# Attention and a gated two-layer network on one core: the last 64 keys of each pair of heads as four products in quarters of the TensorE array

## The chip, the cores and the metric

One core of a Trainium2 chip runs the kernel. The metric is device time in microseconds (us) of one execution, the median of several runs. TensorE does the matrix products (PE in the profile, PEld its weight loads), VectorE is DVE, ScalarE is ACT, GpSimd is POOL, and SyncE (SP) issues the transfers.

## What is computed

Attention over 4 batches, 12 heads, 448 tokens and 64 dimensions a head, with scores capped by tanh, then a network with a cosine gate on the 1792 tokens of 768 features:

```python
scores = scale * np.matmul(q, k.transpose(0, 1, 3, 2))
scores = cap * np.tanh(scores / cap)
scores = scores - np.max(scores, axis=-1, keepdims=True)
attn = np.exp(scores)
attn = attn / (np.sum(attn, axis=-1, keepdims=True) + 1e-09)
out = np.matmul(attn, v)
# heads side by side: x of 1792 x 768
h = x @ w_in                 # 768 x 2048
g = h * np.cos(h)
return g @ w_out             # 2048 x 768
```

## The kernel before

Heads go in pairs: the 64 dimensions of head 0 of a pair lie on partitions 0 to 63, those of head 1 on 64 to 127. Two pairs (a = 0, 1) make a quad q, and there are 12 quads (0 to 11). For each pair one transfer (L320; L125 and L127 for the first quad) brings keys and queries as `qk`, another (L325) the values as `v`. The layout is made on the host in `_layout`.

The 448 keys are cut into groups g of 128, 128, 128 and 64. For the first three, `scores` (L333) makes for each head one product of 64 rows by 128 columns with all 448 queries: the two heads stand in the upper and the lower half of the array's rows, and write two PSUM banks of a tile `pair`. The last 64 keys of both pairs share one tile, `rest`: pair a writes partitions 64a to 64a + 63, head h writes bank h. `scores_rest` (L342) makes its four products each over all 128 rows. For this the 64 keys are stored as 128 columns with zeros: columns 384 to 447 hold head 0 on the upper 64 partitions and zeros below, columns 448 to 511 hold head 1 on the lower 64 and zeros above (KD = 512), so that each product takes the queries of both heads and the zeros remove the wrong one.

From there ScalarE takes the tanh out of PSUM (L352: `t` for the first groups, `late` for rest and the third group) and the exponential in place (L367). VectorE adds the exponentials of a pair up (`sum`, L406, L409, L413). TensorE multiplies them with the values into two tiles `single` (`values`, L426: four column strips of 32, one for each pair and head) and sums them over the keys (`sums`, L435, into a tile `rest`). VectorE then transposes the sums (L446), inverts them (L453), spreads them (L459), scales the result (L463) and splits it into a high and a low part (L466, L469). L426 of the next quad writes the `single` tiles that L463 has read.

In attention the order of every engine is written out: PLAN gives each part a time in a cycle of 13.8, all calls of all quads are sorted by it and made in that order. TensorE does in each quad: scores of pair 0 (groups 0 and 1), `scores_rest`, the values of the rest group of the quad before, scores of pair 1 (groups 0, 1), the sums and the values of group 2 of the quad before, scores of group 2 of both pairs, values of groups 0 and 1. Both `pair` tiles are used in turn; `rest` has one buffer.

During attention the first weights of the network are prepared, in quads 2 to 9: transfers into `w` (L232), and on VectorE in one quad L239, L243, L247, L254, in the next L257, L261 and L476 (the last one in three of them). The network (from L201 on) follows: products of float32r parts into `single` and `pair`, the gate on ScalarE and VectorE, the output product (L611) added to `acc` (L623).

Of the kernel before, what the change touches and what calls it, by code (L numbers as in the profile page):

```python
# [19 lines left out]
B, H, S, D = 4, 12, 448, 64  # L20
# [59 lines left out]
EARLY_AT = dict(no_sign=2.4, scale=2.9, cap=3.4, shift=3.9, tail_bits=16.2, sign_bit=17.1, load=17.2, high=18.1, low=19.8, load_rest=20.0)  # L80
BUSY = 6, 5
PAD = 80
KD = 512
QK = KD + S
Q = slice(KD, QK)
RAW = QK + 128 * NG
# [198 lines left out]
class Heads:  # L285
# [50 lines left out]
    def scores_rest(self, q):  # L336

        ps = self.ps[q] = self.banks.rest()
        for h in range(2):
            for a in range(2):  # L340
                x = self.qk[q, a]
                self.nc.tensor.matmul(ps[64 * a:64 * a + 64, h, 0:S], lhsT=x[:, 384 + 64 * h:448 + 64 * h],  # L342
                                      rhs=x[:, Q], start=True, stop=True)

    def t(self, q, a, g):

# [396 lines left out]
def _layout(inputs):  # L743
    import numpy as np

    q, k, v = inputs['q'], inputs['k'], inputs['v']
    qkv = np.zeros((B, NPAIR, 128, RAW), dtype=q.dtype)
    kt = k.transpose(0, 1, 3, 2).reshape(B, NPAIR, 128, S)
    qkv[..., 0:384] = kt[..., 0:384]
    qkv[:, :, 0:64, 384:448] = kt[:, :, 0:64, 384:448]  # L750
    qkv[:, :, 64:128, 448:512] = kt[:, :, 64:128, 384:448]
    qkv[..., KD:QK] = q.transpose(0, 1, 3, 2).reshape(B, NPAIR, 128, S)
    vp = v.reshape(B, NPAIR, 2, S, D)
    vv = np.zeros((B, NPAIR, 128, NG, 2, D), dtype=v.dtype)
    vv[:, :, :, 0:3] = vp[:, :, :, 0:384].reshape(B, NPAIR, 2, 3, 128, D).transpose(0, 1, 4, 3, 2, 5)
    vv[:, 0::2, 0:64, 3] = vp[:, 0::2, :, 384:448].transpose(0, 1, 3, 2, 4)
    vv[:, 1::2, 64:128, 3] = vp[:, 1::2, :, 384:448].transpose(0, 1, 3, 2, 4)
    qkv[..., QK:RAW] = vv.reshape(B, NPAIR, 128, RAW - QK)
    qkv = qkv.reshape(B * NPAIR, 128, RAW)
    w_in = inputs['moe_w_in'].reshape(NQUAD, 4, 2, 32, DFF).transpose(0, 2, 1, 3, 4)  # L760
    w_in = w_in.reshape(KC, 128, NF, 128).transpose(2, 1, 0, 3).reshape(NF, 128, DM)
    w_out = inputs['moe_w_out'].reshape(NF, 128, DM)
    w_in = np.ascontiguousarray(w_in).view(np.int64)
    w_out = np.ascontiguousarray(w_out).view(np.int64)
    return {'qkv': qkv, 'cap': np.asarray(inputs['cap']).reshape(1), 'w_in': w_in, 'w_out': w_out}
# [24 lines left out]
```

## Time and profile before

| | before |
|---|---|
| time, median of 3 runs | 653.33 us (650.8 to 653.75) |
| profiled execution | 653.35 us |
| its span, first to last instruction | 651.5 us |
| TensorE busy | 640.2 us, 98% |
| VectorE busy | 501.7 us, 77% |
| ScalarE busy | 320.0 us, 49% |
| granted TensorE clock, mean | 0.994 of full |

The profile is one execution. Busy time is that in which an engine has an instruction running; the records of TensorE overlap each other, so the distance between starts tells more than the duration of one. An f32 product shows as two records and two weight loads. "Idle before" is the time in which an engine stood still before an instruction, with what ended it in brackets. Attention ends at about 183 us, the network takes the rest.

### The profile page before, as it was taken

The page shows a single profiled execution, that of the slowest core. Times are in us where ns is not written, and L with a number is a line of the kernel's source. Part 1 is how long each engine was busy: PE and PEld are TensorE (multiplying, and loading weights), DVE is VectorE, ACT ScalarE, POOL GpSimd, SP SyncE. Part 2 cuts the span into 40 slices and gives each one's busy share as a digit, 9 for nine tenths or more (in the row PEclk, how much of TensorE's full clock was granted, in tenths as well). Part 3 has the DMA queues.
Part 4 walks back from the last instruction along what each step waited for, and adds up shares of the span by engine and source line. Part 5 has one row for each costly group of instructions (what it writes and reads, how often), then busy time and mean ns, then how long its engine had stood idle before and what let it go on. Part 6 is the DMA issues. An engine that isn't in the chain of part 4 may idle for free.

```text
span 651.5 us, 9197 instructions
## 1 busy us (share of the span) xinstructions
PE 640.2 (98%) x3755; PEld 498.3 (76%) x3755; DVE 501.7 (77%) x755; ACT 320.0 (49%) x385; POOL 62.1 (10%) x39
## 2 busy tenths in 40 slices
PE   7999999999999999999999999999999999999995
PEld 2333333333469999998999999899999999998995
DVE  1599999997768887877887878777778778777664
ACT  4999999999824333334333333333343333333220
POOL 0001011000011111111111111111111111111000
PEclk9999999999999999999999999999999999999998
DMA  7044342444001122111111221111112211110223
GB/s 262 7 151 140 127 142 94 153 144 144 1 0 50 50 67 79 49 49 48 49 50 51 70 74 50 48 50 49 49 49 66 80 50 49 48 49 1 97 98 150
DMA packets 18497, 49.42 MB, mean 76 GB/s; under 512 B 2192, under 2 KB 2448, under 8 KB 18448
## 3 DMA queue, kind: packets, MB, share of 16 engines
q1 hardware_dynamic: 18448, 48.77, 22.2%
q8 instruction: 31, 0.51, 0.3%
q14 instruction: 18, 0.15, 0.1%
HBM read 43.25 MB, written 5.51 MB: 75 GB/s over the span
## 4 chain that ended last, share of the span: by engine, by line
PE 93%; DVE 3%; ACT 1%; issue 1%; DMA 0%; POOL 0%; ACTq 0%
PE single L201 32%; PE pair L611 24%; PE single L426 12%; PE rest L611 10%; PE pair L333 9%; PE rest L342 3%; PE rest L435 2%; PE pair L201 1%; DVE gl L588 1%; DMA capt<-in_cap_dram 0%; DVE acc L621 0%; DVE y L575 0%; DVE y L582 0%; PE rest L106 0%; POOL wi2l L269 0%
## 5 line engine op out<-in xcount | busy, mean ns | idle before, releaser
L579 ACT ACTIVATE y<-y,angles 128x384 f32<-128x384 f32 (+1 forms) x63 | 42.3, 671 | 161.5 <-DVE y L576 161.5
L623 DVE TENSOR_TENSOR acc<-pair,acc 128x768 f32<-128x768 f32 x70 | 66.7, 953 | 14.3 <-PE pair L611 14.2
L333 PE MATMUL pair<-qk 64*128 64x448 f32 x264 | 58.6, 562 | 0.0
L585 ACT CAST gh<-y 128x384 fp32r<-128x384 f32 (+1 forms) x63 | 35.8, 567 | 45.6 <-DVE y L582 45.6
L582 DVE TENSOR_TENSOR y<-single,y 128x384 f32<-128x384 f32 (+1 forms) x62 | 38.5, 621 | 25.4 <-ACT y L579 25.4
L567 ACT ACTIVATE v<-single,angles 128x384 f32<-128x384 f32 (+1 forms) x62 | 39.0, 629 | 29.0 <-PE single L201 28.9
L236 ACT ACTIVATE u<-w 128x768 f32<-128x768 f32 x28 | 25.1, 895 | 53.9 <-POOL wo2l L269 10.0
L333 PEld LDWEIGHTS pair<-qk 64*128 64x128 f32 x264 | 22.7, 186 | 36.2 <-issue 20.1
L352 ACT ACTIVATE t<-pair,inv 128x896 f32<-128x896 f32 x48 | 45.7, 1004 | 5.8 <-PE pair L333 5.3
L251 DVE TENSOR_SCALAR u<-u 128x768 f32<-128x768 f32 x28 | 15.7, 561 | 39.0 <-ACT u L236 38.9
L367 ACT ACTIVATE t<-t,capt 128x1792 f32<-128x1792 f32 x24 | 42.8, 1783 | 0.4
L406 DVE TENSOR_TENSOR sum<-t 128x896 f32<-128x896 f32 x24 | 26.1, 1088 | 21.2 <-ACT t L367 21.2
L576 DVE SCALAR_TENSOR_TENSOR y<-v,y 128x384 f32<-128x384 f32 (+1 forms) x63 | 39.3, 624 | 2.2
L588 DVE TENSOR_TENSOR gl<-y,gh 128x384 fp32r<-128x384 f32 (+1 forms) x63 | 38.8, 616 | 2.5 <-ACT gh L585 2.5
L426 PE MATMUL single<-late,v 128*32 128x448 f32 x368 | 40.7, 542 | 0.0
L575 DVE SCALAR_TENSOR_TENSOR y<-v,single 128x384 f32<-128x384 f32 (+1 forms) x62 | 38.4, 619 | 2.1
L426 PE MATMUL single<-t,v 128*32 128x448 f32 x368 | 39.2, 546 | 0.0
L570 DVE TENSOR_SCALAR v<-v 128x384 f32<-128x384 f32 (+1 forms) x63 | 24.4, 387 | 15.3 <-ACT v L567 15.2
L201 PE MATMUL single<-xh,wi2l 128*128 128x512 f32 (+1 forms) x96 | 34.9, 363 | 0.0
L201 PE MATMUL single<-xh,wi2h 128*128 128x512 f32 (+1 forms) x96 | 34.8, 363 | 0.0
L201 PE MATMUL single<-xh,wi3h 128*128 128x512 f32 (+1 forms) x96 | 34.7, 362 | 0.0
L201 PE MATMUL single<-xh,wi3l 128*128 128x512 f32 (+1 forms) x96 | 34.7, 362 | 0.0
(151 smaller groups left out, 1571.7 us busy)
## 6 DMA issues: line engine op xcount, KB each, us to landing
w<-in_w_in_dram SPq DMA_DIRECT2D x32, 384.0 KB, 3.6
w<-in_w_out_dram SPq DMA_DIRECT2D x32, 384.0 KB, 3.6
qk<-in_qkv_dram SPq DMA_DIRECT2D x22, 480.0 KB, 4.9
v<-in_qkv_dram SPq DMA_DIRECT2D x23, 256.0 KB, 3.9
out_dram<-acc SPq DMA_DIRECT2D x13, 384.0 KB, 2.3
w<-in_qkv_dram SPq DMA_DIRECT2D x2, 240.0 KB, 3.8
second<-in_qkv_dram SPq DMA_DIRECT2D x1, 480.0 KB, 5.5
out_dram<-acc SPq DMA_DIRECT2D x2, 192.0 KB, 3.9
```

The lines of the kernel that those rows point to most:

```text
L201: nc.tensor.matmul(h[:, 0:n], lhsT=w[:, ks], rhs=x[:, k, toks], start=(k == 0 and i == 0), stop=(k == KC - 1 and i == 2))
L333: self.nc.tensor.matmul(ps[:, h, 0:S], lhsT=x[mine, 128 * g:128 * g + 128], rhs=x[mine, Q], start=True, stop=True)
L352: self.nc.scalar.activation(out, ps[:, :, 0:S], AF.Tanh, scale=self.inv)
L367: self.nc.scalar.activation(t, t, AF.Exp, scale=self.capt)
L426: self.nc.tensor.matmul(self.acc[q][e][o], lhsT=self.v[q, a][:, g, d], rhs=t, start=(g == first), stop=(g == last), tile_position=(0, o.st ...
L567: m.nc.scalar.activation(self.v, self.h, AF.Identity, bias=m.quarter, scale=1.0 / (2.0 * math.pi))
L576: m.nc.vector.scalar_tensor_tensor(self.y, self.v, -TWO_PI_LO, self.y, op0=ALU.mult, op1=ALU.add)
L579: self.m.nc.scalar.activation(self.y, self.y, AF.Sin, bias=self.m.half_pi)
L582: self.m.nc.vector.tensor_mul(self.y, self.h, self.y)
L588: self.m.nc.vector.tensor_sub(self.result(1), self.y, self.result(0))
L611: m.nc.tensor.matmul(y[:, e, 0:HALF], lhsT=x[:, j, toks], rhs=w[:, HALF * e:HALF * e + HALF], start=(j == 0 and k == 0), stop=(j == GF - 1 ...
L623: m.nc.vector.tensor_add(acc, y[:, e, 0:HALF], acc)
```

## The change

`scores_rest` takes for head h only the 64 partitions of that head, for the keys and for the queries, and names the place in the array: rows 64h, columns 64a. The keys of a pair are stored once, without zeros (KD = S = 448), so a pair's keys and queries are 896 words a partition instead of 960. The order of the calls stays.

```diff
-KD = 512
+KD = S
 QK = KD + S
 Q = slice(KD, QK)
 RAW = QK + 128 * NG
...
         for h in range(2):
             for a in range(2):
-                x = self.qk[q, a]
-                self.nc.tensor.matmul(ps[64 * a:64 * a + 64, h, 0:S], lhsT=x[:, 384 + 64 * h:448 + 64 * h],
-                                      rhs=x[:, Q], start=True, stop=True)
+                x, mine = self.qk[q, a], slice(64 * h, 64 * h + 64)
+                self.nc.tensor.matmul(ps[64 * a:64 * a + 64, h, 0:S], lhsT=x[mine, 384:448], rhs=x[mine, Q],
+                                      start=True, stop=True, tile_position=(64 * h, 64 * a))
...
-    qkv[..., 0:384] = kt[..., 0:384]
-    qkv[:, :, 0:64, 384:448] = kt[:, :, 0:64, 384:448]
-    qkv[:, :, 64:128, 448:512] = kt[:, :, 64:128, 384:448]
+    qkv[..., 0:KD] = kt
```

## Rows read from the trace of the kernel before

**Rows 1.** Page, part 1: busy time, share of the span, instructions.
```profile
PE 640.2 (98%) x3755; PEld 498.3 (76%) x3755; DVE 501.7 (77%) x755; ACT 320.0 (49%) x385; POOL 62.1 (10%) x39
```

**Rows 2.** Page, part 4: the chain that ended last, shares by line.
```profile
PE single L201 32%; PE pair L611 24%; PE single L426 12%; PE rest L611 10%; PE pair L333 9%; PE rest L342 3%; PE rest L435 2%; PE pair L201 1%; DVE gl L588 1%; DMA capt<-in_cap_dram 0%; DVE acc L621 0%; DVE y L575 0%; DVE y L582 0%; PE rest L106 0%; POOL wi2l L269 0%
```

**Rows 3.** Stretches: length, busy PE, PEld, DVE, ACT, POOL (instructions), clock, DMA share, GB/s.
```profile
77.40:91.40 14.00, 14.00 (x110) 4.60 (x106) 13.14 (x19) 12.96 (x12) 2.68 (x1) 1.00 0.32 105
91.40:105.30 13.90, 13.90 (x108) 4.57 (x104) 12.81 (x20) 12.90 (x11) 0.00 (x0) 1.00 0.48 173
...
161.10:175.00 13.90, 13.90 (x108) 4.58 (x104) 10.69 (x16) 12.92 (x11) 0.00 (x0) 1.00 0.01 2
...
190.00:640.00 450.00, 449.68 (x2425) 427.91 (x2424) 348.96 (x537) 158.67 (x244) 52.85 (x29) 1.00 0.17 56
```

**Rows 4.** Timeline, TensorE: start, duration (us), line, out<-in, shape, count [idle before].
```profile
100.48 1.77 PE L333 MATMUL pair<-qk 64*128 64x448 f32 x8
102.19 3.21 PE L426 MATMUL single<-t,v 128*32 128x448 f32 x32
...
107.04 1.73 PE L342 MATMUL rest<-qk 128*64 128x448 f32 x8
108.69 1.71 PE L426 MATMUL single<-late,v 128*32 128x448 f32 x16
...
112.04 0.96 PE L435 MATMUL rest<-sum,one 128*32 128x448 f32 x8
...
114.43 1.77 PE L333 MATMUL pair<-qk 64*128 64x448 f32 x8
```

**Rows 5.** Timeline, TensorE, L342 in the first quad.
```profile
9.74 0.59 PE L342 MATMUL rest<-w 128*64 128x448 f32 x1
9.74 0.59 PE L342 MATMUL rest<-second 128*64 128x448 f32 x1
10.16 0.54 PE L342 MATMUL rest<-w 128*64 128x448 f32 x1
...
10.54 0.54 PE L342 MATMUL rest<-w 128*64 128x448 f32 x1
```

**Rows 6.** Timeline, TensorE, L426 in the first quad (values of two pairs).
```profile
20.05 0.54 PE L426 MATMUL single<-t,u 128*32 128x448 f32 x2
20.07 0.54 PE L426 MATMUL single<-t,v 128*32 128x448 f32 x2
20.43 0.54 PE L426 MATMUL single<-t,u 128*32 128x448 f32 x2
```

**Rows 7.** TensorE's weight loads: L426 in the timeline; L342 by line (min/median/max ns).
```profile
103.34 0.13 PEld L426 LDWEIGHTS single<-t,v 128*32 128x32 f32 x4 [0.25 <-issue]
...
L342 PEld LDWEIGHTS rest<-qk x88: 132/137/137, 23.4 to 163.6; 128*64 128x64 f32 x88
```

**Rows 8.** Timeline, ScalarE: its two waits in one quad.
```profile
108.81 1.01 ACT L352 ACTIVATE late<-rest,inv 128x896 f32<-128x896 f32 x1 [0.50 <-PE rest L342]
...
115.50 1.01 ACT L352 ACTIVATE late<-pair,inv 128x896 f32<-128x896 f32 x1 [0.37 <-PE pair L333]
```

**Rows 9.** Timeline, VectorE, in a quad that ends a weight piece.
```profile
100.83 1.16 DVE L463 TENSOR_TENSOR x<-single,s 128x448 f32<-128x448 f32 x2
...
111.53 1.09 DVE L406 TENSOR_TENSOR sum<-t 128x896 f32<-128x896 f32 x1
113.06 0.65 DVE L446 STREAM_TRANSPOSE s<-rest 128x448 f32<-128x448 f32 x1 [0.44 <-PE rest L435]
...
114.78 1.16 DVE L463 TENSOR_TENSOR x<-single,s 128x448 f32<-128x448 f32 x2
```

**Rows 10.** Timeline, VectorE, in the quad before, which begins a weight piece.
```profile
95.80 0.56 DVE L239 TENSOR_SCALAR u<-w 128x768 int32<-128x768 int32 x1 [0.64 <-DMA w<-in_w_out_dram]
...
99.12 0.65 DVE L446 STREAM_TRANSPOSE s<-rest 128x448 f32<-128x448 f32 x1
```

**Rows 11.** Timeline, ScalarE, in the first quad.
```profile
11.51 1.01 ACT L352 ACTIVATE late<-rest,inv 128x896 f32<-128x896 f32 x1 [0.52 <-PE rest L342]
```

## Prediction

> **What bounds the kernel now.** I read the busy shares first: TensorE is busy 98% of the span [rows 1]. A busy matmul engine proves little, so next comes the chain that ended last: the reader should see there that nearly all of it is TensorE's own lines, and that the line which the change rewrites, L342, holds 3% of the span [rows 2]. The table of stretches says where another engine stands close behind [rows 3]. In attention, from 21.6 to 175.0, TensorE is busy for the whole of every stretch, and ScalarE is busy some 12.9 of 13.9 us; VectorE is at 12.8 to 13.1 in the quads that also prepare weights, and at 10.7 in the last ones. In the second half (190 to 640) TensorE is busy 449.68 of 450 us, and VectorE 349. So whatever attention saves moves the second half forward whole, and the question is only what attention saves.
>
> Then one quad on TensorE in order of time [rows 4]. From the third pair of scores of one quad (100.48) to that of the next (114.43) it takes 13.95 us, the same for quads 1 to 11 within 0.01 us. Within it, no line shows an idle time: TensorE sets this beat alone. L342 takes 107.04 to 108.69 = 1.65 us of it, as 8 records (each f32 product shows as two).
>
> **The new product.** The first quad has its two key loads under different names, so its records stand apart [rows 5]: the product from pair 0 and that from pair 1 start together at 9.74, and their second halves at 10.16; then come 10.54 and so on. So the two column halves of the array run side by side, four rounds of two records, 0.38 us a round. The first round is 0.42, and the last, up to the next line's start, 0.47: 0.42 + 2 x 0.38 + 0.47 = 1.65, as in the steady quad. After the change each product needs 64 rows only, so the two heads can run side by side too: two rounds of four records. L426 does four records side by side already, in four column strips (20.05 and 20.07 hold two each, the next round starts 0.38 later) [rows 6], and L333 two in row halves: 8 records in 1.70 us [rows 4]. Both directions at once is what no row shows. Taken together they leave 0.42 + 0.47 = 0.89 instead of 1.65: two rounds less, 0.75 us a quad. At the worst that rows price, all four products follow each other (8 rounds, 1.5 us more a quad); at the best the entry and exit extras (0.04 and 0.09) go too, another 0.1. I take 0.75, since each direction alone keeps the full round of 0.38 with as many records as there are tiles. The head is also the index of the PSUM bank in this line, so the two row halves write different banks, as in L333, and nothing new meets there.
>
> A page speaks against this. In L426 the four products of a round share all the rows, and yet the weights of the next round load while they run: four loads of together 0.13 us, begun 0.25 us after the last ones [rows 7], with the rounds still 0.38 apart. The Trainium skill, "TensorE: Matmul & The Clock Gate", section "Part 3: Packing small matmuls — row/col tiling", says that a weight load overlaps running matmuls only if its row group differs. By that rule the two products of one head would not overlap; the sum by it is the slower rival below, and the sum by rows is the 0.75. The trace does not agree with the rule for column strips.
>
> **What else changes.** The key loads shrink by a fifteenth (from 960 to 896 words a row). TensorE waits for none of them in attention, so this is worth nothing on the path; it can only help a late weight transfer behind them. The tile order, the plan and all waits of the engines stay. No instruction is added or taken away; L342 keeps its 8 records, 4 products and their loads.
>
> **What comes next on the path.** TensorE's beat becomes 13.95 - 0.75 = 13.20 us. ScalarE waits 0.50 us for L342 and 0.37 for the third pair of scores in each quad [rows 8]; the first wait goes (L342's result comes 0.75 earlier, ScalarE is free 0.50 earlier), and the second shrinks as ScalarE gains 0.50 and TensorE 0.75. It needs no more than 13.95 - 0.87 = 13.08, less than 13.20: not the bound, by 0.1 us.
>
> VectorE is the nearest. In a quad that ends a weight piece [rows 9], L463 ends at 100.83 + 1.16 = 101.99 and lets L426 start at 102.19. From there VectorE has no idle time until L406 ends at 111.53 + 1.09 = 112.62; it then waits 0.44 for the sums (L435) and starts L446 at 113.06, 1.02 after L435 began at 112.04. From L446 to the next end of L463 (114.78 + 1.16 = 115.94) takes 2.88. With the wait gone, its beat is 13.95 - 0.44 = 13.51, that is 0.31 more than TensorE's new one. Three quads are like this. In the four that begin a piece VectorE is busy 0.3 us less in a stretch 0.1 us shorter [rows 3], so about 13.25, 0.05 over. The 0.20 us between L463's end and L426 is slack, spent once; some of it is the way of the signal, so I take 0.15. VectorE thus takes back 3 x 0.31 + 4 x 0.05 - 0.15 = 0.98 us over the kernel. Once L426 waits for L463, all of TensorE's queue waits behind it.
>
> In one quad VectorE also waited 0.64 us for a weight transfer, so that L446 at 99.12 came without any wait for TensorE [rows 10]. That transfer is issued behind the values of the quad before, so it keeps its distance to the beat: there the quad cannot get shorter by more than the slack, and 0.58 of its 0.75 are lost. This depends on when one transfer lands: 0 if it lands as early as in the other quads, and with smaller transfers ahead of it. I take 0.4.
>
> The first quad is set by ScalarE, which waits 0.52 us for L342 [rows 11]. What it gains there lies between 0 and 0.52, since TensorE may hold it up later in the same quad. I take 0.3, about the middle.
>
> **The sum.** 11 x 0.75 = 8.25, plus 0.3 for the first quad, minus 0.98 and 0.4: 7.2 us. The profiled execution took 653.35 us (651.5 of span and 1.85 around it); the median of the runs is 653.33, so nothing is to be corrected. 653.35 - 7.2 = 646.2.
>
> **The rivals.**
> First, only two tiles run at a time, so four rounds stay: the change does not do what it says. For it speaks only that no row shows both directions at once; against it, that each works fully by itself. 653.3 us, within 0.5% of before for sure. Chance 0.08.
>
> Second, on the other side: products that share their rows follow each other, weights included. Then each row half has four records of 0.38, each with its own load of 0.14 (the median of L342's loads, [rows 7]). 4 x 0.52 = 2.08, plus 0.09 at the exit, 2.17 against 1.65: 0.52 more in each of 12 quads, 6.2 us, 659.6. It decides as soon as a group takes longer than 1.65 us, that is with fewer than two products at a time. Against it: the four strips of L426, which share their rows and run together [rows 6, 7]. That is the rule of the page named above. Chance 0.05.
>
> Third, VectorE takes back far more: every quad that begins a weight piece gets the late transfer (4 x 0.58 = 2.3 in place of 0.2 + 0.4), and the extras at the change of tile shape grow by 0.1 in each quad (1.2). 7.2 - 1.7 - 1.2 = 4.3: 649.0. For it: VectorE's 13.51 is over the new beat already. Against it: only one of the four waited. Chance 0.09.
>
> The forecast itself gets the rest, 0.78.
>
> **How the numbers follow.** The forecast's own range goes from all gains and no loss (8.25 + 0.52 + 11 x 0.1 = 9.9, 643.5) to the loss of the transfer in a second quad (647). To hold 8 in 10 the range takes in the third case too: 643.5 to 649.5, leaving out the first two rivals and a little more. A measurement of this kernel can tell about 0.5%, 3.3 us, from no change; faster by more is below 650.1. Forecast and third rival lie below it: 0.86. Within 0.5% is the first rival and a few mixtures: 0.09. Slower is the second: 0.05.
>
> **What would show it.** In the profile after, L342's eight records should start in two rounds of four, 0.4 us apart, with 0.9 us to the next line; four rounds would be the first rival, more than 1.65 us the second. ScalarE's 0.50 before the tanh of L342 should be gone. The wait of VectorE's L446 for L435 should vanish in the weight quads and stay in the last two quads. TensorE should show short waits for L463 at the start of L426 in quads 3 to 9 and nowhere else; quads 10 and 11 should take 13.20 us each. The second half should keep its length. If the last quads too are longer than 13.2, or TensorE waits for ScalarE, the account of the engines behind it was wrong.

## The result and the profile after

The changed kernel takes 643.88 us (median of 4 runs, 642.73 to 643.93); the kernel before, in the same measurement, 652.08 (650.8 to 653.75). The ratio is 0.987, with a 95% interval of 0.985 to 0.989. The interval leaves out 1, so it is faster, and by a little more than the 7.2 us of the forecast: the medians are 8.2 us apart. The profiled executions, which the account below adds up, are 653.35 and 643.93 us, 9.4 apart; their spans are 651.47 and 642.14, 9.3 apart.

TensorE in one quad of the changed kernel, as in [rows 4] (start, duration, line, out<-in, shape, count):

```profile
95.73 1.77 PE L333 MATMUL pair<-qk 64*128 64x448 f32 x8
97.43 3.21 PE L426 MATMUL single<-t,v 128*32 128x448 f32 x32
...
102.28 0.98 PE L342 MATMUL rest<-qk 64*64 64x448 f32 x8
103.19 1.71 PE L426 MATMUL single<-late,v 128*32 128x448 f32 x16
...
108.93 1.77 PE L333 MATMUL pair<-qk 64*128 64x448 f32 x8
110.64 0.58 PE L426 MATMUL single<-t,v 128*32 128x448 f32 x4
```

L342 now takes 102.28 to 103.19 = 0.91 us instead of 1.65, and the quad 95.73 to 108.93 = 13.20 instead of 13.95. There is still no idle time on TensorE in this quad. The first quad shows the rounds one by one, as in [rows 5]; the timeline of TensorE again:

```profile
9.75 0.59 PE L342 MATMUL rest<-w 64*64 64x448 f32 x1
9.75 0.59 PE L342 MATMUL rest<-second 64*64 64x448 f32 x1
9.76 0.59 PE L342 MATMUL rest<-w 64*64 64x448 f32 x1
9.77 0.59 PE L342 MATMUL rest<-second 64*64 64x448 f32 x1
10.17 0.54 PE L342 MATMUL rest<-w 64*64 64x448 f32 x1
...
10.66 1.77 PE L333 MATMUL pair<-second 64*128 64x448 f32 x8
```

Four records start within 0.02 us, the second four 0.42 later, and the next line 0.49 after that. So the quarters do run four at a time. ScalarE's wait for L342 [rows 8] is gone, and its second wait is down from 0.37 to 0.25 (ScalarE's timeline):

```profile
103.44 1.01 ACT L352 ACTIVATE late<-rest,inv 128x896 f32<-128x896 f32 x1
...
110.00 1.01 ACT L352 ACTIVATE late<-pair,inv 128x896 f32<-128x896 f32 x1 [0.25 <-PE pair L333]
```

VectorE, in the quad that answers to [rows 9] and in the one before it (VectorE's timeline):

```profile
91.31 0.57 DVE L239 TENSOR_SCALAR u<-w 128x768 int32<-128x768 int32 x1
...
96.29 1.16 DVE L463 TENSOR_TENSOR x<-single,s 128x448 f32<-128x448 f32 x2
...
106.46 0.56 DVE L476 CAST wo0h<-u 128x768 fp32r<-128x768 f32 x1
106.93 1.08 DVE L406 TENSOR_TENSOR sum<-t 128x896 f32<-128x896 f32 x1
107.93 0.65 DVE L446 STREAM_TRANSPOSE s<-rest 128x448 f32<-128x448 f32 x1
...
109.64 1.16 DVE L463 TENSOR_TENSOR x<-single,s 128x448 f32<-128x448 f32 x2
...
122.78 1.16 DVE L463 TENSOR_TENSOR x<-single,s 128x448 f32<-128x448 f32 x2
```

L446 no longer waits for the sums: VectorE is behind TensorE in this quad, as forecast. But TensorE does not wait for it. The pair of L463 ends at 109.64 + 1.16 = 110.80, and L426 had started at 110.64, before that end. In the kernel before it started 0.20 after it ([rows 4, 9]). This row contradicts the prediction's account of what L426 waits for, and the experiments start from it. L239, which waited 0.64 for its transfer [rows 10], shows no wait here.

The second half kept its length: from the first product of the network to the end of the last addition it is 470.6 us before (from 175.06) and after (from 166.59). Within it the engines are as busy as before (stretches: length, busy PE, PEld, DVE, ACT, POOL, clock, DMA share, GB/s; compare [rows 3]):

```profile
180.00:630.00 450.00, 449.71 (x2424) 427.99 (x2423) 347.79 (x535) 159.82 (x246) 53.62 (x29) 1.00 0.17 56
```

### The profile page after: what moved, and what is told of

It reads as the page before. It is cut to its first block, busy times and chain, and to the rows that moved or that the text cites. A ratio compares the mean times of both kernels' runs of the same rounds, so it can differ in the third digit from the quotient of the medians.

```text
span 642.1 us, 9197 instructions
## 1 busy us (share of the span) xinstructions
PE 631.8 (98%) x3755; PEld 495.9 (77%) x3755; DVE 500.5 (78%) x755; ACT 318.5 (50%) x385; POOL 61.9 (10%) x39
## 4 chain that ended last, share of the span: by engine, by line
PE 93%; DVE 3%; ACT 2%; issue 1%; DMA 0%; POOL 0%; ACTq 0%
PE single L201 32%; PE pair L611 24%; PE single L426 12%; PE rest L611 10%; PE pair L333 9%; PE rest L435 2%; PE rest L342 2%; PE pair L201 1%; DVE gl L588 1%; DMA capt<-in_cap_dram 0%; ACT t L352 0%; DVE acc L621 0%; DVE y L575 0%; DVE y L582 0%; PE rest L106 0%
## 5 line engine op out<-in xcount | busy, mean ns | idle before, releaser
L333 PE MATMUL pair<-qk 64*128 64x448 f32 x264 | 58.6, 562 | 0.0
L333 PEld LDWEIGHTS pair<-qk 64*128 64x128 f32 x264 | 22.8, 186 | 36.1 <-issue 19.8
L426 PE MATMUL single<-late,v 128*32 128x448 f32 x368 | 40.7, 542 | 0.0
L406 DVE TENSOR_TENSOR sum<-t 128x896 f32<-128x896 f32 x24 | 26.0, 1085 | 18.1 <-ACT t L367 18.1
L426 PE MATMUL single<-t,v 128*32 128x448 f32 x368 | 39.6, 548 | 0.0
L201 PE MATMUL single<-xl,wi3h 128*128 128x512 f32 (+1 forms) x96 | 34.7, 362 | 0.0
```

Source lines behind the costliest of these rows:

```text
L201: nc.tensor.matmul(h[:, 0:n], lhsT=w[:, ks], rhs=x[:, k, toks], start=(k == 0 and i == 0), stop=(k == KC - 1 and i == 2))
L333: self.nc.tensor.matmul(ps[:, h, 0:S], lhsT=x[mine, 128 * g:128 * g + 128], rhs=x[mine, Q], start=True, stop=True)
L426: self.nc.tensor.matmul(self.acc[q][e][o], lhsT=self.v[q, a][:, g, d], rhs=t, start=(g == first), stop=(g == last), tile_position=(0, o.st ...
```

## The experiments

**Products alone, products in another order.** The first kernel keeps the old layout with zeros and the transfers of 960 words (its edits against the changed kernel, the lines of `_layout` left out):

```diff
-KD = S
+KD = 512
...
-                self.nc.tensor.matmul(..., lhsT=x[mine, 384:448], rhs=x[mine, Q],
+                self.nc.tensor.matmul(..., lhsT=x[mine, 384 + 64 * h:448 + 64 * h], rhs=x[mine, Q],
```

> The products in quarters alone: keys are stored with the zeros as before (960 words a row, KD = 512), and the products take only their 64 rows. If the whole gain is TensorE's two rounds a quad: L342's group 0.91 us, 13.20 us a quad, the network begins at 166.6, the time within 1 us of the changed kernel (643.9). If the smaller transfers carry part of it: VectorE's L239 waits again for a weight transfer (0.4 to 0.6 us in one quad) and the slack of L463 ahead of L426 shrinks there by as much; the time still moves only when that slack (0.37 us at the least in the changed kernel) is used up, so at most 0.3 us.

Measured: 643.55 us (641.11 to 643.93), ratio 0.985 (0.982 to 0.988); L342's group 0.91 us; from the values of the second quad to those of the last, 30.99 to 163.01, ten quads of 13.20; no wait of L239. The whole gain is the products'; the smaller transfers carry none of it that can be seen.

The second exchanges the loops:

```diff
-        for h in range(2):
-            for a in range(2):
+        for a in range(2):
+            for h in range(2):
```

> The four products in another order: pairs outside, heads inside, so that products of one column half and different row halves follow each other. If a tile of the array runs as soon as its own predecessor is done, whatever stands between: L342's group stays at 0.91 us, two rounds of four. If four at a time needs products with the same rows to be neighbours: more than two rounds, 1.3 us (three) to 1.65 us (four), and 0.4 to 0.75 us more a quad, 4.5 to 9 us in all.

Measured: 643.52 us, L342's group 0.91 us. The four run at a time in both orders. TensorE's timeline in the first quad of that kernel:

```profile
10.35 0.59 PE L342 MATMUL rest<-w 64*64 64x448 f32 x2
10.37 0.59 PE L342 MATMUL rest<-second 64*64 64x448 f32 x2
10.78 0.54 PE L342 MATMUL rest<-w 64*64 64x448 f32 x2
```

This run also gave, by chance, a late transfer like the one that the prediction priced at 0.58 us, though L239 waits 0.22 for it here and not 0.64. VectorE's timeline, and under it TensorE's:

```profile
91.18 0.57 DVE L239 TENSOR_SCALAR u<-w 128x768 int32<-128x768 int32 x1 [0.22 <-DMA w<-in_w_out_dram]
...
109.49 1.16 DVE L463 TENSOR_TENSOR x<-single,s 128x448 f32<-128x448 f32 x2
```
```profile
96.95 3.21 PE L426 MATMUL single<-t,v 128*32 128x448 f32 x32
...
110.17 3.31 PE L426 MATMUL single<-t,v 128*32 128x448 f32 x32
...
123.47 1.71 PE L426 MATMUL single<-t,v 128*32 128x448 f32 x16
```

The transfer came later than in the changed kernel, VectorE fell further behind (L426 starts 0.48 before the end of the pair of L463: 109.49 + 1.16 = 110.65 against 110.17), and the quads at 96.95 and 110.17 took 13.22 and 13.30. So this late transfer costs some 0.1 us, because there is slack to take the rest of it.

**How much slack, and where.** L463 is one row of two instructions, one for each of the two `single` tiles. If L426's first products wait only for the tile they write, the slack counts from the end of the first L463: in the changed kernel and before, where VectorE is on time, 0.73 us (the second ends 0.53 later, and 0.20 before L426). To use the slack up, VectorE gets more work in the four quads that begin a weight piece:

```diff
+        at(CYCLE * cycle + EARLY_AT["no_sign"], calls["no_sign"])
```

> L239 (0.56 us on VectorE, with its step 0.59) made twice in each of the four quads that begin a weight piece. Theory: L426's first products wait only for the first of the two L463, so TensorE has 0.73 us of slack, of which some 0.03 is the way of the signal. VectorE's beats are 13.17 + 0.59 in these quads and 13.35 in the three that end a piece with L476, against 13.20: 4 x 0.56 + 3 x 0.15 - 0.70 = 2.0 us later at the start of the network. The prediction's account (slack 0.15, beats 13.25 + 0.59 and 13.51): 4 x 0.64 + 3 x 0.31 - 0.15 = 3.3 us. If VectorE doesn't bound these quads at all: 0.

Measured, TensorE's timeline with the values of the second, a middle and the last quad, then VectorE's at the middle one:

```profile
31.01 3.21 PE L426 MATMUL single<-t,v 128*32 128x448 f32 x32
...
71.20 3.31 PE L426 MATMUL single<-t,v 128*32 128x448 f32 x32 [0.41 <-DVE x L463]
...
165.15 3.21 PE L426 MATMUL single<-t,v 128*32 128x448 f32 x32
```
```profile
70.53 1.16 DVE L463 TENSOR_TENSOR x<-single,s 128x448 f32<-128x448 f32 x2
```

The same two rows of the changed kernel:

```profile
31.42 3.21 PE L426 MATMUL single<-t,v 128*32 128x448 f32 x32
...
163.45 3.21 PE L426 MATMUL single<-t,v 128*32 128x448 f32 x32
```

The ten quads took 165.15 - 31.01 = 134.14 against 132.03: 2.1 us longer, where the theory said 2.0 and the prediction's account 3.3. (The prediction's slack of 0.15 with the theory's beats, which are nearer to those measured, would give 4 x 0.56 + 3 x 0.15 - 0.15 = 2.5, so the length alone does not decide on the slack; the moment at which L426 starts does.) Now TensorE waits for L463, and even then it starts at 71.20, 0.49 before the pair ends (70.53 + 1.16 = 71.69): the first of the two ended at 71.15. The whole kernel took 645.21 us in its one run.

To see that it is the tile written first that counts, the two L463 were exchanged on top of this:

```diff
-    ("norm_scale", (0,), 21.2),
-    ("norm_scale", (1,), 21.8),
+    ("norm_scale", (1,), 21.2),
+    ("norm_scale", (0,), 21.8),
```

> As e4_no_sign_twice, and the two L463 of a quad in the other order, so that the tile that L426 writes first is freed by the second of them. Theory (the slack is that of the tile written first): the slack falls from 0.73 to 0.20 us, so the network begins 0.5 us later than in e4_no_sign_twice, 2.5 later than in the changed kernel. If L426 waits for both L463 anyhow, as the prediction took it, the order makes no difference: as e4_no_sign_twice within 0.1 us.

Measured: 164.92 - 30.85 = 134.07, the same as before the exchange (the whole kernel 645.70 us in its one run). The theory's 0.5 us did not come. TensorE's timeline and then VectorE's at the middle quad:

```profile
71.03 3.31 PE L426 MATMUL single<-t,v 128*32 128x448 f32 x32 [0.40 <-DVE x L463]
```
```profile
70.35 1.16 DVE L463 TENSOR_TENSOR x<-single,s 128x448 f32<-128x448 f32 x2
```

L426 again starts 0.48 before the pair ends (71.51), as without the exchange. The likely reason is that the pool, which hands out the PSUM banks of the tiles, gave the bank that is freed first to the tile that is written first, so that the two tiles changed banks from quad to quad. No trace names the banks; the next run tests it. So this run does not tell the two accounts apart. With each tile held on its own bank:

```diff
-        return self.pool.tile([128, 512], F32, name="single", tag="single")
+        self.made = 1 - getattr(self, "made", 1)
+        return self.pool.tile([128, 512], F32, name="single", tag=f"single{self.made}", bufs=1)
```

> As e3_twice_swapped, but each of the two single tiles keeps its PSUM bank from quad to quad (in e3_twice_swapped the pool gave the bank freed first to the tile written first, whichever it was, so the swap changed nothing). Now L426's first products write the bank that the second L463 frees. Theory (the slack is that of the bank written first): 0.20 us in place of 0.73, L426 never starts before the end of the second L463, and the quads from the first L426 to the last take together 0.5 us more than in e4_no_sign_twice (2.1 us over ten times 13.20 there, 2.6 here). If L426 needs both tiles anyhow: no difference from e4_no_sign_twice.

Measured (this kernel has one line more, so L426 is L427, L463 is L464 and L333 is L334), TensorE's timeline and then VectorE's at the middle quad:

```profile
28.49 3.22 PE L427 MATMUL single<-t,v 128*32 128x448 f32 x32
...
69.20 3.33 PE L427 MATMUL single<-t,v 128*32 128x448 f32 x32 [0.36 <-PE pair L334]
...
163.10 3.25 PE L427 MATMUL single<-t,v 128*32 128x448 f32 x32
```
```profile
67.95 1.15 DVE L464 TENSOR_TENSOR x<-single,s 128x448 f32<-128x448 f32 x2
```

163.10 - 28.49 = 134.61: 0.5 us more than in e4, as the theory said. L427 now starts at 69.20, 0.10 after the second L464 (67.95 + 1.15 = 69.10), never ahead of it. (The whole kernel took 643.30 us in its one run; that is shorter than e4's because its second quad starts some 2.5 us earlier, for which see the last section.) The row names L334 as what ended the wait, but L334 is the line whose products had just run on TensorE itself; the end of L464 is what fits the start. So the slack is that of the bank written first, shown from both sides: 0.73 us from the end of the first L463, of which 0.05 stayed unused in e4.

**A step further.** Of TensorE's beat of 13.20, what is not rounds of products is the extra time at each change of tile shape. The values of the rest group can stand beside the sums, so that three groups in column strips follow each other:

```diff
-    ("values", (3,), 14.4),
+    ("values", (3,), 18.4),
```

This is e5; in e6 the time is 18.55, just behind the sums.

> The changed kernel again, on the same chip as the two that follow: 643.9 us.

> A step further: the values of the rest group are moved from behind L342 to just ahead of the sums (time 18.4 in place of 14.4), so that three groups of products in column strips follow each other and one change of tile shape a quad falls away. The group takes 1.64 us alone, four rounds within others 1.50: 0.14 us a quad, 1.6 us in all, if TensorE sets the beat (13.06). VectorE's beats of 13.35 and 13.17 in seven quads are over that by 0.29 and 0.11: 3 x 0.29 + 4 x 0.11 = 1.3, less 0.7 of slack, so 0.6 us comes back as waits for L463. Together 1.0 us less than the changed kernel.

> The same move to just behind the sums (18.55): the sums come 1.5 us earlier than in e5_values_before_sums, so in quads without weights VectorE's L446 waits for its own work and not for L435, and the slack of L463 grows from 0.7 to about 1.0 us. Then 1.6 less some 0.3 of waits: 1.3 us less than the changed kernel. Against it: the sums also need VectorE's last addition (L409), which ends only 0.2 to 0.3 us before; if VectorE is late, TensorE waits there, and it is no better than e5_values_before_sums.

Measured on one chip: the changed kernel 642.92 us (ratio to before 0.986, 0.984 to 0.988), e5 642.85 (0.985, 0.983 to 0.987), e6 642.35 (0.984, 0.983 to 0.986). The three intervals overlap, so neither step is shown to be faster. The trace shows why so little can be there. TensorE in e5, at two quads:

```profile
78.89 1.77 PE L333 MATMUL pair<-qk 64*128 64x448 f32 x8
80.74 3.31 PE L426 MATMUL single<-t,v 128*32 128x448 f32 x32
...
92.20 1.77 PE L333 MATMUL pair<-qk 64*128 64x448 f32 x8
93.90 3.30 PE L426 MATMUL single<-t,v 128*32 128x448 f32 x32
```

The group before L426 takes 1.85 us at 78.89 instead of 1.70: L426 waits for L463 here. Quads without weights take 13.06 to 13.07, as forecast. So do the first two with weights, until the slack is used up; the others take 13.15 to 13.36. From the second quad's values to the last's, e5 takes 131.38 us, e6 131.44 and the changed kernel 132.03: 0.6 us gained in ten quads, of the 1.4 that the fewer changes of shape are worth. In e6 the forecast of less waiting was wrong: its slack of 1.0 us is there only in the quads after the weights, 0.7 ahead of them, and the weight quads took back the same. VectorE sets the beat in those quads now.

## Why the prediction was right or wrong

**Direction and main term: right.** Two rounds of four records, 0.91 us against a forecast of 0.89, 0.74 us a quad against 0.75. From L333 of the second quad to the first product of the network that is 8.16 us against 8.25. That the two directions of packing add up was the one thing no row showed, and it held in full; both the first rival (four rounds stay) and the second (slower) are out. For the second the row of the weight loads is the plainest. TensorE's loads in the changed kernel:

```profile
102.28 0.21 PEld L342 LDWEIGHTS rest<-qk 64*64 64x64 f32 x8 [0.65 <-issue]
```

All eight loads of the group are done within 0.21 us, though in each half of the rows four of them share their rows, and the first products start at 102.28 too and run on to the next round, 0.42 later. By the rule of the Trainium skill ("TensorE: Matmul & The Clock Gate", "Part 3: Packing small matmuls — row/col tiling") that a load overlaps running products only if its row group differs, these loads would have waited; the trace does not agree with it here. The same section also lets a load go ahead when it targets the background weight buffer, and that the trace does not contradict.

**First quad: right in size.** From L333 of the second quad on, TensorE is 0.3 us earlier beyond the main term (21.36 against 21.67), as taken. But this stretch moves by more than that between executions (last section), so the agreement says little.

**VectorE takes 0.98 us back: wrong, 0.** This is the step that failed, in both of its parts. The wait was wrong: "L463 ends at 101.99 and lets L426 start at 102.19". The row has two instructions, and L426 needs only the first of them for its first products, so the slack was 0.73 and not 0.20. The beats were too long: 13.51 was read as 13.95 less the wait, but L406 starts 0.09 before the end of L476 and L446 0.08 before the end of L406 once none of them waits, and the quad took 109.64 - 96.29 = 13.35. The quad after it, which begins a weight piece, took 122.78 - 109.64 = 13.14 against a forecast of 13.25; that is less than TensorE's 13.20, so VectorE catches up there.

The beats were the larger part of the error. By the prediction's beats VectorE would have fallen 3 x 0.31 + 4 x 0.05 = 1.13 us behind; in the trace its lag never passed 0.36. With that lag the prediction's slack of 0.15 would have left some 0.2 us to take back, an estimate from these numbers; the slack of 0.73 makes it nothing. The waits of TensorE for L463, which the prediction named as its sign, are in no quad of the changed kernel, and appear as soon as VectorE is given more work (e4).

**The late transfer takes 0.4 us back: wrong, 0.** The transfer came in time in this execution; in e2 one was late and cost 0.1. The same slack takes up the rest.

**Not in the sum at all: the end.** The last addition ends 0.9 us closer to the end of the span than before: 636.18 + 1.02 to 642.1 is 4.9 us, 644.65 + 1.02 to 651.5 was 5.8. In between lies only the last transfer of the output, and the changed kernel measured again has 4.05. So it moves by as much between executions of one kernel, and the edit touches nothing there. That the change has no part in it is still argued, not shown: the kernel before has one trace, and its 5.8 is longer than in all nine others (4.05 to 5.25). With 8.16 and 0.3 it makes up the 9.3 between the spans. The medians, 8.2 apart, are close to the main term alone; the larger distance of the two profiled executions is in part luck.

**The third rival** (649.0, VectorE and dearer changes of shape) fails by the same step as the term, and its dearer changes of shape did not come either: the group of L342 takes 0.02 more than the rounds forecast, not 0.1. The forecast of 646.2 was thus too slow by about the 1.4 us that it gave to VectorE and the transfer, and by the end of the span.

## What to carry to other kernels

Where TensorE sets the beat and half of a product's rows are zeros, cutting it into quarters of the array is worth a try: here four went side by side, their weight loads too, in both orders tried, and the group fell from 1.65 to 0.91 us. When the engine behind the bound comes near, ask of the row that frees a buffer how many instructions it holds and which of them the next product really needs; with two buffers the slack is that of the one written first. And read an engine's beat from rows in which it does not wait, since its instructions can stand closer there. An exchange of two steps may change nothing where a pool decides which buffer a tile gets: hold the tiles in place before concluding from it.

## What the runs showed beyond that

The kernel's own start varies more than most of the experiments' edits are worth. In the first quad the clock of TensorE is at its lower level (1.2 GHz) for 3.4 us in some executions and not at all in others. Stretches of the changed kernel and, below, of e5:

```profile
15.90:19.30 3.40, 3.40 (x18) 1.29 (x18) 1.09 (x1) 3.37 (x3) 0.00 (x0) 0.51 0.00 0
```
```profile
15.90:19.30 3.40, 3.40 (x30) 1.14 (x24) 1.73 (x3) 3.34 (x4) 0.00 (x0) 1.00 0.00 0
```

TensorE had waited 2.02 us for ScalarE shortly before in the changed kernel, and 2.19 in e5, so that wait alone does not decide. The lower level is not the larger part either: the changed kernel measured again has full clock in this stretch, and its second quad starts at 20.83, only 0.5 earlier. In e5 the first scores already ran at full rounds (8 records in 1.70 us from 5.98, against 2.72 from 7.03), and the second quad started at 18.41 instead of 21.36. That is 3 us, of which e5's edit explains none: e7, which does not have that edit, started as early. What decides how early the start runs at full rounds was not tried.
